# Layernorm, 32-head attention and a gated GLU on one core: Q and K projected in 120-row tiles and laid out through DRAM, and a freer choice of banks for side work

## The chip, the cores and the metric

The kernel runs on one core of one Trainium2 chip. The metric is the device time in microseconds, given as the median of three runs. Engines are named as in the profile: PE (matmuls), PEld (weight loads of PE), DVE (vector), ACT (scalar), POOL (GpSimd), SP (the engine that issues most DMAs).

## What is computed

```
xn = layernorm(x)                            # x: 2048 x 640
q, k, v = split(xn @ wqkv)                   # 32 heads of 20 columns
s = (softmax(q k^T / sqrt(20)) v) @ wo       # per head, 2048 queries by 2048 keys
g = silu((sigmoid(xn @ w_gate) * (xn @ w_up)) @ w_down)     # F = 1728
out = x + s * g
```

All inputs are bfloat16.

## The kernel before

**Blocks.** The 32 heads form 8 groups of 4, and the 2048 queries 4 chunks of 512: 32 blocks (`b`), worked through in order. In a block each of the 4 heads meets 16 key tiles of 128, so there are 64 jobs. A job is a score matmul (L559, `score_mm`; the four heads stand on four 32-row strips of PE, so up to four run beside each other), an exponential, and a value matmul (L599, into `oacc`; the heads stand on four 32-column strips).

**Two ways to the exponential.** Most jobs go to ACT (L83, `pt`), two or three score tiles at a time, from `scA0` or `scA1` (two banks each) and, for a third tile, from `bank[0]` or `bank[1]`. Some key tiles go to DVE, all four heads together: `iv` (L844, one per head, from a bank) and then four integer passes `pb` (L644), whose value matmuls use four scaled copies of V (`v`, `vs`).

**Side work on PE.** Between scores and values PE does everything else: K of the next group (`mk_k`, L354), Q of the next block (`mk_q`, L365, with the bound below, L168), V (`mk_v`, L385), the GLU (`mk_gu` L415, `mk_down` L438) and the output projection (`mk_out`, L475, only in the last blocks). Each is an `Item`: PE steps into one of the single banks, then ACT and DVE steps that read it and set the bank free. Their order is written out by a planner inside the kernel (the `while` loop in L778): it walks through an assumed time, keeps what each engine is busy with, and lets a score step, a value step or a side step be next by rules in L902 to L915. Side work takes `bank[2]`, and the two others only while it is behind a due amount (L886 to L890). `URGENT`, `ROUNDS`, `HOLD`, `SLACK`, `LEAD`, `LAG`, `D_LAST` in L29 are numbers of these rules. PE, ACT and DVE run in exactly this order; SP and POOL instructions are put in order by the framework.

**Q and K.** Four heads of 20 columns are spread to 4 x 32 columns, so that each head starts on a strip: POOL copies the weights into `wqk` (L120) with zeros in between, and a projection of a group has 128 output rows, 80 of them filled. Column 0 of each strip carries a bound: K has 1 there (`ones_r`), and Q gets minus the sum of |q| times the largest |k| of each row, by one more matmul (L168) of `aq` = |q| (ACT, L164) with `md`, which comes from the maxima of K (`k_max`, L150). DVE evacuates K into `kT` (L144) and Q into a `q` tile (L172), both in SBUF and ready for the scores.

**After a block.** DVE copies `oacc` to `on` (L612); the row sums go through DRAM (`ld`, `lt`, DVE `rt`, `rd`, `rl`, all issued by SP), POOL multiplies (`on_bf`, L629), and SP writes the heads' rows into `oU` (L637). The gate results leave DVE in two buffers `gqs` (L448) and are written to DRAM.

**End.** When all items are done, `tail_steps` projects the last 512 rows and writes them out.

Of the kernel before, what the change touches and what calls it, by code (L numbers as in the profile page):

```python
# [18 lines left out]
P = 128  # L19
# [33 lines left out]
def kernel(  # L53
# [41 lines left out]
    gq_dram = dram.tile([S, D], FP32, name="gq_dram", tag="gqd", bufs=1)  # L95

# [5 lines left out]
    wqks = [persist.tile([P, 2 * KD, GH, 32], BF16, name=f"wqk{i}") for i in range(2)]  # L102
# [5 lines left out]
    eps_t = const.tile([P, 1], FP32, name="eps_t")  # L108
    mds = [const.tile([P, P], BF16, name=f"md{i}") for i in range(2)]
# [6 lines left out]
    def load_wqk(g):  # L116
        st = wk.tile([P, KD, 2, GC], BF16, tag="wst", bufs=2, name="wst")
# [8 lines left out]
    def load_wv(pr):  # L126
        w = wk.tile([P, KD, 2 * GC], BF16, tag="wv", bufs=2, name="wv")
        nc.sync.dma_start(out=w, in_=wqkv_v[:, :, 2, pr * 2 * GC:(pr + 1) * 2 * GC])
        return w
# [32 lines left out]
    def q_abs(ps):  # L162
        aq = wk.tile([P, QC], BF16, tag="aq", bufs=1, name="aq")
        nc.scalar.activation(out=aq, in_=ps, func=ACT.Abs)  # L164
        return aq
# [4 lines left out]
    def q_evac(ps):  # L170
        q = wk.tile([P, QC], BF16, tag="q", bufs=3, name="q")
        nc.vector.tensor_scalar_mul(out=q, in0=ps, scalar1=qscale)  # L172
        return q
# [7 lines left out]
    def v_evac(ps, pr, tts):  # L181
        n = len(tts)
        src = ps[:, 0:n * 2 * GC].rearrange("p (t h e) -> p t h e", t=n, e=DH)
        nc.vector.tensor_copy(out=vts[pr % 2][:, tts[0]:tts[0] + n, :, 1:1 + DH], in_=src)
        for i, tt in enumerate(tts):
            if tt in DKT:
                vf = wk.tile([P, 2 * GC], FP32, tag="vf", bufs=2, name="vf")
# [9 lines left out]
    with tc.tile_pool(name="ln", bufs=2) as lp, \  # L197
# [17 lines left out]
        for j in range(GH):  # L215
# [6 lines left out]
                                base=31, pattern=[[32, GH], [P, 32]], channel_multiplier=-1)  # L222
        for i in range(2):
# [5 lines left out]
        aq0 = q_first = psq = None  # L229
# [36 lines left out]
        q_first = q_evac(psq)  # L266
# [47 lines left out]
    qs = {0: q_first}  # L314
# [42 lines left out]
    def mk_q(b, at):  # L357
# [13 lines left out]
        def ev():  # L371
            qs[b] = q_evac(st["ps"])
# [3 lines left out]
                     ("DVE", 0.60, ev, "free", lambda t: q_at.__setitem__(b, t))], at, pre=[("md", g)])  # L376

# [123 lines left out]
    for b in range(NBLK):  # L501
        g, c = divmod(b, NQC)
        mk = []
        if g + 1 < NG:
            mk.append(lambda at, g=g, c=c: [mk_k(g + 1, c, at)])
        if g % 2 == 1 and g + 1 < NG:
# [6 lines left out]
        if b + 1 < NBLK:  # L513
            mk.insert(min(1, len(mk)), lambda at, b=b: [mk_q(b + 1, at)])
# [43 lines left out]
    def score_mm(dst, b, kt, j):  # L558
        nc.tensor.matmul(dst, lhsT=kTs[(b // NQC) % 2][32 * j:32 * j + 32, kt * P:(kt + 1) * P],  # L559
                         rhs=qs[b][32 * j:32 * j + 32, :], start=True, stop=True, tile_position=(32 * j, 0))  # L560
# [58 lines left out]
    def norm_b(b, on, lt):  # L619
# [5 lines left out]
        rl = w2.tile([P, QC], FP32, tag="rl", bufs=2, name="rl")  # L625
# [38 lines left out]
    def tail_steps():  # L664
# [27 lines left out]
        early(mains[3], 3, slice(0, 512), False)  # L692
        tp2 = psum.tile([P, 2 * QC], BF16, name="tp2", tag="oacc")
        for i in range(4):
            nc.tensor.transpose(out=tp2[0:GC, i * P:(i + 1) * P], in_=onq[:, i, :], identity=ident)
        o7 = w2.tile([GC, QC], BF16, tag="on_bf", bufs=2, name="o7")
# [29 lines left out]
    with tc.manual_schedule(engines={ENG.PE, ENG.Activation, ENG.DVE}):  # L726
# [21 lines left out]
        active = []  # L748
        norm_pending = None
# [28 lines left out]
        while pv_block[0] < NBLK or items or glu_items or any(it.i < len(it.ops) for it in active):  # L778
# [3 lines left out]
            if bb > blk_loaded:  # L782
                blk_loaded = bb
                g, c = divmod(bb, NQC)
                if c == 0 and g + 1 < NG:
                    load_wqk(g + 1)
# [5 lines left out]
            active = [it for it in active if it.i < len(it.ops)]  # L792

# [77 lines left out]
            if free["PE"] <= now:  # L871
# [10 lines left out]
                if cur is None:  # L882
                    m_new, m_bank = None, None
# [22 lines left out]
                elif can_f and (margin < URGENT or stay is None):  # L906
# [9 lines left out]
                if nxt == "F":  # L916
# [3 lines left out]
                    d_bank = None  # L920
                    if d_can and busy <= T_F + T_MODE + PL + SLACK:
                        d_bank = next((f for f in (2, (nfill + 1) % 2, nfill % 2) if flex[f] <= now), None)
# [104 lines left out]
```

## Time and profile before

| what | value |
|---|---|
| median of three runs | 928.38 us (926.77 to 932.43) |
| the profiled execution | 926.63 us, its span 924.8 us |
| mean granted TensorE clock | 0.982 |
| PE, ACT, DVE busy | 852.2, 828.1, 751.3 us |
| POOL busy | 103.8 us |
| DMA | 54.28 MB, mean 59 GB/s |

Busy time is the time in which at least one instruction of the engine was under way. Instructions of PE and of ACT overlap, so the time of one instruction is longer than what it adds; the distance from one start to the next is what it costs in a dense stretch. In a group of instructions the row gives its line, engine, operation, output and inputs, count, busy time, mean length, then the idle time of the engine ahead of them and what ended it.

### The profile page before, as it was taken

The numbers are of one execution on the slowest core, as the hardware profiler recorded it, in microseconds if no ns is written. First come the engines' busy times: TensorE is split into PE (matmuls) and PEld (weight loads), VectorE is DVE, ScalarE is ACT, GpSimd is POOL, SyncE is SP. The second block draws the span as 40 slices with busy tenths as digits, with TensorE's granted clock in tenths as the row PEclk, the third lists the DMA queues.
The fourth block names the chain that finished last, engine by engine and source line by source line (L and its number), as shares of the span: only waits on it lengthen the run. The fifth ranks groups of instructions, "written<-read, shape, count | busy, mean of one in ns | idle before, by whom it ended". The sixth has DMA issues, their size and how long they took to land.

```text
span 924.8 us, 18739 instructions
## 1 busy us (share of the span) xinstructions
PE 852.2 (92%) x7266; PEld 294.5 (32%) x7352; DVE 751.3 (81%) x1288; ACT 828.1 (90%) x1037; POOL 103.8 (11%) x138
## 2 busy tenths in 40 slices
PE   3799999999999999999999999999999999889875
PEld 2332223343322233333222333333323333223222
DVE  8588758888778997887859888899897688998864
ACT  3799999999999999998999999999999999998760
POOL 3020100111000000111000000111000000003222
PEclk9799999999999999999999999999999999999898
DMA  8402222112121221101221211101211111213431
GB/s 224 136 11 63 63 66 62 39 32 56 43 73 35 66 62 38 32 25 29 63 73 37 74 34 36 39 13 46 62 46 38 31 39 31 93 38 112 137 96 55
DMA packets 85288, 54.28 MB, mean 59 GB/s; under 512 B 33172, under 2 KB 79060, under 8 KB 85200
## 3 DMA queue, kind: packets, MB, share of 16 engines
q1 hardware_dynamic: 83760, 51.45, 19.8%
q10 hardware_dynamic: 1440, 1.64, 0.5%
q8 instruction: 57, 0.93, 0.4%
q14 instruction: 31, 0.25, 0.1%
HBM read 42.15 MB, written 8.37 MB: 55 GB/s over the span
## 4 chain that ended last, share of the span: by engine, by line
PE 49%; ACT 23%; DVE 18%; issue 6%; DMA 2%; SPq 1%; POOL 0%; DVEq 0%; ACTq 0%; POOLq 0%
PE oacc L599 13%; PE scA_431 L559 7%; PE scA_430 L559 6%; DVE pb L644 6%; DVE iv L844 6%; PE bk_434 L415 4%; PE bk_432 L415 3%; PE bk_433 L415 3%; PE bk_433 L438 2%; PE bk_432 L438 1%; PE bk_434 L475 1%; PE bk_434 L438 1%; PE bk_432 L365 1%; PE bk_434 L354 1%; DVE stats L236 1%
## 5 line engine op out<-in xcount | busy, mean ns | idle before, releaser
L644 DVE TENSOR_SCALAR pb<-iv 128x2048 int16<-128x2048 int16 x440 | 304.1, 715 | 2.8
L844 DVE TENSOR_SCALAR iv<-bk_434 128x512 int16<-128x512 f32 x182 | 124.5, 684 | 39.8 <-PE bk_434 L559 39.4
L844 DVE TENSOR_SCALAR iv<-bk_433 128x512 int16<-128x512 f32 x131 | 89.4, 683 | 29.6 <-PE bk_433 L559 29.3
L844 DVE TENSOR_SCALAR iv<-bk_432 128x512 int16<-128x512 f32 x127 | 86.6, 682 | 23.1 <-PE bk_432 L559 22.8
L629 POOL TENSOR_TENSOR on_bf<-on,rl 128x512 bf16<-128x512 f32 x31 | 42.7, 1378 | 537.0 <-DMA rl<-rd 365.4
L599 PE MATMUL oacc<-pb,vs_74 128*21 128x512 bf16 x684 | 86.8, 392 | 2.8 <-DVE pb L644 2.6
L559 PEld LDWEIGHTS <-kT_69 32*128 32x128 bf16 x1024 | 38.4, 91 | 130.0 <-issue 125.3
L559 PEld LDWEIGHTS <-kT_70 32*128 32x128 bf16 x1024 | 40.1, 91 | 124.0 <-issue 117.5
L559 PE MATMUL scA_430<-q,kT_69 32*128 32x512 bf16 x367 | 73.3, 386 | 2.9 <-DVE q L172 0.8
L559 PE MATMUL scA_431<-q,kT_70 32*128 32x512 bf16 x362 | 71.1, 385 | 4.0 <-ACT pt_10982 L83 0.7
L559 PE MATMUL scA_430<-q,kT_70 32*128 32x512 bf16 x357 | 71.0, 386 | 3.2 <-ACT pt_10810 L83 0.5
L559 PE MATMUL scA_431<-q,kT_69 32*128 32x512 bf16 x359 | 71.1, 385 | 1.8 <-ACT pt_1526 L83 0.3
L599 PE MATMUL oacc<-pb,vs_73 128*21 128x512 bf16 x636 | 70.4, 381 | 0.5 <-issue 0.3
L415 PE MATMUL bk_434<-xnT,wgu 128*128 128x512 bf16 (+1 forms) x224 | 68.4, 383 | 1.2 <-issue 0.8
L415 PEld LDWEIGHTS <-wgu 128*128 128x128 bf16 (+1 forms) x560 | 43.3, 98 | 75.8 <-issue 54.0
L438 PEld LDWEIGHTS <-hT 128*128 128x128 bf16 x448 | 35.9, 97 | 46.8 <-issue 38.1
L415 PE MATMUL bk_432<-xnT,wgu 128*128 128x512 bf16 (+1 forms) x155 | 47.6, 383 | 2.0 <-DVE iv L844 1.0
L599 PEld LDWEIGHTS <-v_72 128*21 128x21 bf16 x1024 | 31.4, 91 | 47.5 <-issue 36.8
L559 PE MATMUL bk_433<-q,kT_70 32*128 32x512 bf16 x114 | 44.4, 389 | 0.1
L415 PE MATMUL bk_433<-xnT,wgu 128*128 128x512 bf16 (+1 forms) x142 | 42.8, 383 | 1.9 <-issue 0.8
L559 PE MATMUL bk_433<-q,kT_69 32*128 32x512 bf16 x108 | 41.6, 385 | 0.0
L559 PE MATMUL bk_432<-q,kT_69 32*128 32x512 bf16 x103 | 39.9, 388 | 0.0
(1780 smaller groups left out, 2150.4 us busy)
## 6 DMA issues: line engine op xcount, KB each, us to landing
rl<-rd SPq DMA_DIRECT2D x124, 64.0 KB
wgu<-in_B_w_gate_dram SPq DMA_DIRECT2D x24, 320.0 KB
wgu<-in_B_w_up_dram SPq DMA_DIRECT2D x24, 320.0 KB
gq_dram<-gqs SPq DMA_DIRECT2D x32, 160.0 KB
ob<-gq_dram SPq DMA_DIRECT2D x12, 320.0 KB
oU<-on_bf SPq DMA_DIRECT2D x108, 20.0 KB
wd<-in_B_w_down_dram SPq DMA_DIRECT2D x1, 2080.0 KB
ob<-in_A_x_dram SPq DMA_DIRECT2D x12, 160.0 KB
```

Source lines behind the costliest of these rows:

```text
L236: nc.vector.bn_stats(out=stats[:, h, :], in_=xt[:, i, h * HD:(h + 1) * HD])
L354: nc.tensor.matmul(ps, lhsT=wslice(g, 1, kd), rhs=xnT[:, kd, c * 512:(c + 1) * 512], start=(kd == 0), stop=(kd == KD - 1))
L365: nc.tensor.matmul(st["ps"], lhsT=wslice(g, 0, kd), rhs=xnT[:, kd, c * QC:(c + 1) * QC], start=(kd == 0), stop=(kd == KD - 1))
L415: nc.tensor.matmul(st[key][0:fs, :], lhsT=w[:, i, kd, ko * P:ko * P + fs], rhs=xnT[:, kd, c * QC:(c + 1) * QC], start=(kd == 0), stop=(kd ...
L438: nc.tensor.matmul(st["ps"][:, 0:HD], lhsT=hT[0:fsz[kf], kf, t4 * P:(t4 + 1) * P], rhs=wd[0:fsz[kf], kf, h * HD:(h + 1) * HD], start=(kf = ...
L475: nc.tensor.matmul(st["ps"][:, 0:HD], lhsT=oU[:, kd, tt * P:(tt + 1) * P], rhs=wo[:, kd, h * HD:(h + 1) * HD], start=(kd == 0), stop=(kd = ...
L559: nc.tensor.matmul(dst, lhsT=kTs[(b // NQC) % 2][32 * j:32 * j + 32, kt * P:(kt + 1) * P], rhs=qs[b][32 * j:32 * j + 32, :], start=True, s ...
L599: nc.tensor.matmul(oacc[32 * j:32 * j + DH + 1, :], lhsT=lhsT, rhs=u["src"], start=first, stop=last, tile_position=(0, 32 * j), skip_group ...
L629: nc.gpsimd.tensor_tensor(out=on_bf, in0=on, in1=rl, op=ALU.mult)
L644: nc.vector.tensor_scalar(out=pb[:, k, :, :].bitcast(I16), in0=iv, scalar1=0.25, scalar2=cst, op0=ALU.mult, op1=ALU.add)
L844: nc.vector.tensor_scalar(out=d["iv"][:, j, :], in0=bank[bk], scalar1=I_OFF, scalar2=I_LOW, op0=ALU.add, op1=ALU.max)
```

## The change

Groups 0 and 1 (heads 0 to 7) keep the old way. Heads 8 to 31 form four units `u` of six heads, 120 columns. The weights of a unit are loaded as they are (`load_wu`, no copy on POOL). K of a chunk (`mk_ku`) and Q of a chunk (`mk_qu`) are projected into 120 rows, evacuated by DVE into a small tile (`ku`, `qu`, one ring of two buffers) and written to DRAM (`kD`, `qD`). The bounds of a unit, for all four chunks, come from four matmuls into four 32-column strips of one bank (`mk_bu`), and go to DRAM too (`bD`). `load_kT` and `load_q` then read each head's 20 rows to their strip in `kT` and in one of three fixed `q` tiles. The numbers of the planner change, side work may take any bank once all scores are claimed or when neither a value nor a score step is possible (`FALL`), and in `tail_steps` a transpose moves ahead of five matmuls and four additions move back. Some buffers shrink from two to one (`wst`, `wv`, `vf`, `rl`).

```diff
-URGENT, ROUNDS, HOLD, SLACK, LEAD, LAG, D_LAST, D_LAST_END = 0.15, 3, 0.15, 0.8, 40.0, 8.0, 16, 0
+PG = 2
+UH = 6
+UC = UH * DH
+
+URGENT, ROUNDS, HOLD, SLACK, LEAD, LAG, D_LAST, D_LAST_END = 0.15, 4, 0.0, 0.1, 20.0, -5.0, 20, 0
+D_ORD, M_ORD, WAIT3, FALL = 0, 1, 0.0, 1
...
+    qts = [persist.tile([P, QC], BF16, name=f"q{i}") for i in range(3)]
...
-        aq = wk.tile([P, QC], BF16, tag="aq", bufs=1, name="aq")
+        aq = wk.tile([P, QC], BF16, tag="aq", bufs=4, name="aq")
...
+    def load_wu(u):
+        w = wk.tile([P, 2 * KD, GH, 32], BF16, tag="wp", bufs=2, name="wu")
...
+        for i in range(2):
+            nc.sync.dma_start(out=w[:, :, i, :], in_=wqkv_v[:, :, i, f0:f0 + UC])
...
+    def mk_ku(u, c, at):
...
+        def ev():
+            st["k"] = wk.tile([P, QC], BF16, tag="ku", bufs=2, name="ku")[0:UC, :]
+            nc.vector.tensor_copy(out=st["k"], in_=st["ps"][0:UC, :])
+            nc.sync.dma_start(out=kD[u][:, c * QC:(c + 1) * QC], in_=st["k"])
...
+        return Item([("PE", alloc, [(T_MM, lambda kd=kd: u_mm(st, u, 1, c, kd)) for kd in range(KD)]),
+                     ("DVE", 0.60, ev, "free", mark("kD", u, c)), ("DVE", 0.60, mx, "", end)], at,
+                    pre=[("wu", u)])
...
+    def mk_qu(u, c, at):
...
+            q = wk.tile([P, QC], BF16, tag="ku", bufs=2, name="qu")[0:UC, :]
+            nc.vector.tensor_scalar_mul(out=q, in0=st["ps"][0:UC, :], scalar1=qscale)
+            nc.sync.dma_start(out=qD[u][:, c * QC:(c + 1) * QC], in_=q)
...
+    def mk_bu(u, at):
...
+            for c in range(NQC):
+                nc.tensor.matmul(st["ps"][32 * c:32 * c + UH, :], lhsT=mku[u][2], rhs=aqs[(u, c)][0:UC, :],
+                                 start=True, stop=True, tile_position=(0, 32 * c), skip_group_check=True)
...
+            bt = wk.tile([P, QC], BF16, tag="ku", bufs=2, name="bt")
...
+    def load_kT(g):
+        for u, o, j, n in spans(g):
+            for i in range(n):
+                r = 32 * (j + i) + 1
+                nc.sync.dma_start(out=kTs[g % 2][r:r + DH, :], in_=kD[u][(o + i) * DH:(o + i + 1) * DH, :])
...
+    def load_q(b):
...
+                nc.sync.dma_start(out=qts[b % 3][r:r + DH, :], in_=qD[u][(o + i) * DH:(o + i + 1) * DH, cs])
+            nc.sync.dma_start(out=heads(qts[b % 3])[j:j + n, 0, :], in_=bD[u][o:o + n, cs])
...
+        for u in range(NU):
+            first = (PG + u * UH // GH - 1) * NQC
+            if first <= b < first + 3:
+                if b == first:
+                    mk.append(lambda at, u=u: [mk_ku(u, i, at) for i in range(NQC)])
+                if b == first + 1:
+                    mk.append(lambda at, u=u: [mk_qu(u, i, at) for i in range(NQC)] + [mk_bu(u, at)])
...
-        early(mains[3], 3, slice(0, 512), False)
         tp2 = psum.tile([P, 2 * QC], BF16, name="tp2", tag="oacc")
         for i in range(4):
             nc.tensor.transpose(out=tp2[0:GC, i * P:(i + 1) * P], in_=onq[:, i, :], identity=ident)
+        early(mains[3], 3, slice(0, 512), False)
...
+            if k_next < NG and base() >= (k_next - 1) * NQC and all(
+                    ev_at.get(("kD", u, c), 1e9) <= now for u, _, _, _ in spans(k_next) for c in range(NQC)):
+                load_kT(k_next)
+                k_at[k_next] = now + 5.5
...
+            if q_next < NBLK and base() >= q_next - 2:
...
+                    load_q(q_next)
+                    q_at[q_next] = max(now + 5.0, k_at[q_next // NQC])
...
-                        for f in ((2, (nfill + 1) % 2, nfill % 2) if behind else (2,)):
+                        for f in ((2,) if not behind and claimed[0] < NJOB * NBLK and not (FALL and not pv_ok and not can_f) else [(2, 1 - own, own), (2, own, 1 - own)][M_ORD]):
```

In the changed file the score matmul is L689, the value matmul L729, the unit's projection L402, its bounds L462, the evacuations of K, Q and bounds L413, L448 and L467, the writes L414, L449 and L469, the reads of K L490 and of Q L498 and L499, and the output projection L598.

On PE, early in the program, before: a projection of K for group 1 (`wqk`, 128 output rows) between value weights and values. Each matmul has its weight load in the row above it.

```order
L385 LDWEIGHTS xnT
L385 MATMUL bk_433<-wv,xnT 128x160
L354 LDWEIGHTS wqk_76
L354 MATMUL bk_434<-xnT,wqk_76 128x512
L354 LDWEIGHTS wqk_76
L354 MATMUL bk_434<-xnT,wqk_76 128x512
```

And now, in block 4, the first projection of unit 0 (`wu`, 120 output rows), with a score step in its midst:

```order
L402 LDWEIGHTS wu
L402 MATMUL bk_451<-xnT,wu 120x512
L402 LDWEIGHTS wu
L402 MATMUL bk_451<-xnT,wu 120x512
L689 LDWEIGHTS kT_82
L689 MATMUL scA_449<-q_95,kT_82 128x512
L689 LDWEIGHTS kT_82
L689 MATMUL scA_449<-q_95,kT_82 128x512
L689 LDWEIGHTS kT_82
L689 MATMUL bk_450<-q_95,kT_82 128x512
L402 LDWEIGHTS wu
L402 MATMUL bk_451<-xnT,wu 120x512
```

The step itself is the same; there are fewer of them, and K of six heads goes into a bank that then leaves for DRAM instead of `kT`.

On SP, where block 3 has ended and `ld`, `lt`, `rd`, `rl` and `oU` carry its row sums, with the writes of K of unit 0 now among them and the reads into `kT` behind them:

```order
L744 DMA ld<-on 4x512
L746 DMA lt<-ld 128x16
L414 DMA kD_67<-ku 120x512 x2
L754 DMA rd<-rt 128x16
L414 DMA kD_67<-ku 120x512
L757 DMA rl<-rd 32x512 x4
L414 DMA kD_67<-ku 120x512
L767 DMA oU<-on_bf 20x512 x4
L490 DMA kT_81<-kD_67 20x2048 x4
```

Before, a block's queue held these rows (here from block 4's `rl` to block 5's `lt`) with at most writes of `gqs` and loads of weights among them:

```order
L627 DMA rl<-rd 32x512 x4
L450 DMA gq_dram<-gqs 128x320
L637 DMA oU<-on_bf 20x512 x2
L637 DMA oU<-on_bf 8x512
L637 DMA oU<-on_bf 12x512
L637 DMA oU<-on_bf 20x512
L450 DMA gq_dram<-gqs 128x320
L614 DMA ld<-on 4x512
L450 DMA gq_dram<-gqs 128x320
L616 DMA lt<-ld 128x16
```

The writes of K stand in the same queue as the row sums, and each is released by DVE's evacuation.

On PE, at the end of the last block, before: the last value matmuls (`pt`, ACT's exponentials) and behind them output projections, all into `bk_434` (32 of them in this way).

```order
L599 LDWEIGHTS v_72
L599 MATMUL oacc<-pt_11783,v_72 21x512
L475 LDWEIGHTS oU
L475 MATMUL bk_434<-wo,oU 128x320
L475 LDWEIGHTS oU
L475 MATMUL bk_434<-wo,oU 128x320
```

And now, with the last DVE tile's values (`pb`) and 13 output projections behind them, in banks `bk_452`, `bk_451` and `bk_450`:

```order
L729 LDWEIGHTS vs_86
L729 MATMUL oacc<-pb,vs_86 21x512
L598 LDWEIGHTS oU
L598 MATMUL bk_452<-wo,oU 128x320
L598 LDWEIGHTS oU
L598 MATMUL bk_452<-wo,oU 128x320
L598 LDWEIGHTS oU
L598 MATMUL bk_452<-wo,oU 128x320
L598 LDWEIGHTS oU
L598 MATMUL bk_451<-wo,oU 128x320
```

More of the output projections have moved ahead of the last values, and the rest no longer share one bank.

More of the change, by code (lines that the diff above doesn't have):

```diff
@@ new lines, with alloc, ab, ev @@
+    aqs = {}
+    def mk_qu(u, c, at):
+        st = {}
+        def alloc():
+            st["ps"] = misc_ps()
+        def ab():
+            aqs[(u, c)] = q_abs(st["ps"])
+        def ev():
+            q = wk.tile([P, QC], BF16, tag="ku", bufs=2, name="qu")[0:UC, :]
+            nc.vector.tensor_scalar_mul(out=q, in0=st["ps"][0:UC, :], scalar1=qscale)
+            nc.sync.dma_start(out=qD[u][:, c * QC:(c + 1) * QC], in_=q)
+        return Item([("PE", alloc, [(T_MM, lambda kd=kd: u_mm(st, u, 0, c, kd)) for kd in range(KD)]),
+                     ("ACT", 0.48, ab, "", mark("aq", u, c)),
+                     ("DVE", 0.60, ev, "free", mark("qD", u, c))], at, pre=[("bD", u - 1)] if u else [])
@@ L695, in tail_steps @@
             nc.tensor.transpose(out=tp2[0:GC, i * P:(i + 1) * P], in_=onq[:, i, :], identity=ident)
+        early(mains[3], 3, slice(0, 512), False)
+        o7 = w2.tile([GC, QC], BF16, tag="on_bf", bufs=2, name="o7")
+        nc.vector.tensor_copy(out=o7, in_=tp2[0:GC, 0:QC])
+        for t4 in range(4):
+            late_mm(mains[t4], t4, slice(0, 512))
+        rest = bank[2]
+        for t4 in range(4):
+            dst = rest[:, t4 * EX:(t4 + 1) * EX]
+            early(dst, t4, slice(512, D), False)
+            late_mm(dst, t4, slice(512, D))
@@ L905 @@
                     nxt = "PV"
-                elif can_f and (margin < URGENT or stay is None):
+                elif can_f and (margin < URGENT or (stay is None and not (flex[nfill % 2] <= now + WAIT3 and flex[nfill % 2] > now and margin > WAIT3))):
                     nxt = "F"
```

162 lines of the change are left out of this document (143 added, 19 removed).

## The prediction, made before the changed kernel ran

> **What bounds the kernel now.** I read the busy shares first, then the slices, then busy time by stage, then single rows for what one step costs.
>
> ```profile
> PE 852.2 (92%) x7266; PEld 294.5 (32%) x7352; DVE 751.3 (81%) x1288; ACT 828.1 (90%) x1037; POOL 103.8 (11%) x138
> ...
> PE   3799999999999999999999999999999999889875
> ...
> ACT  3799999999999999998999999999999999998760
> PEclk9799999999999999999999999999999999999898
> ```
>
> No engine stands out. PE is at 90% or more in slices 3 to 34, ACT in slices 3 to 36 but one, and both fall off after that. By stage (columns: window, its length, then busy us of PE, PEld, DVE, ACT, POOL, granted clock, DMA share, GB/s):
>
> ```profile
> 500.00:600.00 100.00, 97.41 (x875) 34.09 (x881) 85.68 (x146) 97.33 (x124) 7.10 (x8) 1.00 0.14 42
> 100.00:766.00 666.00, 645.44 (x5558) 220.80 (x5628) 550.62 (x919) 637.52 (x797) 58.20 (x67) 1.00 0.17 47
> 766.00:794.00 28.00, 25.46 (x223) 7.85 (x222) 23.95 (x43) 25.13 (x32) 1.26 (x1) 0.94 0.28 90
> 794.00:816.00 22.00, 18.89 (x179) 5.63 (x179) 21.21 (x36) 21.84 (x29) 1.64 (x1) 1.00 0.11 29
> 816.00:890.00 74.00, 63.59 (x575) 20.70 (x574) 64.54 (x107) 64.89 (x77) 17.73 (x19) 0.93 0.32 98
> ```
>
> From 100 to 766 PE is 96.9% busy and ACT 95.7%. From 794 to 816 PE has almost no side work left: PE falls to 86% and ACT rises to 99.3%. So ACT can run nearly without gaps when PE has time to spare; where PE is full, ACT's gaps are scores that come late. From 100 to 890 ACT is busy 637.52 + 25.13 + 21.84 + 64.89 = 749.4 of 790 us: 40.6 us of gaps is what a lighter PE could win back.
>
> A matmul's busy time overstates PE, so I take its cost from the distance between starts (start, length, instruction):
>
> ```profile
> 299.58 1.04 PE L415 MATMUL bk_434<-xnT,wgu 128*128 128x512 bf16 x4
> 300.55 0.39 PE L559 MATMUL scA_431<-q,kT_69 32*128 32x512 bf16 x2
> ...
> 301.78 0.59 PE L599 MATMUL oacc<-pt_3858,v_72 128*21 128x512 bf16 x3
> 302.00 0.38 PE L599 MATMUL oacc<-pt_3868,v_72 128*21 128x512 bf16 x2
> 302.21 0.38 PE L599 MATMUL oacc<-pt_3895,v_72 128*21 128x512 bf16 x2
> ...
> 302.53 0.39 PE L559 MATMUL scA_431<-q,kT_69 32*128 32x512 bf16 x2
> ...
> 302.85 0.39 PE L599 MATMUL oacc<-pb,v_72 128*21 128x512 bf16 x2
> ```
>
> Four projections take 1.04 us, the last of them about 0.38: (1.04 - 0.38)/3 = 0.22 us a step. Value steps (up to four beside each other) start at 301.78, 302.00 and 302.21: 0.22 again. From scores to values, 302.53 to 302.85, it is 0.32: a change of kind costs 0.10 more.
>
> ACT in the same way:
>
> ```profile
> 299.87 0.62 ACT L164 ACTIVATE aq<-bk_433 128x512 bf16<-128x512 f32 x1
> 300.34 1.05 ACT L83 ACTIVATE pt_3895<-scA_430 128x1024 bf16<-128x1024 f32 x1
> 301.25 1.07 ACT L83 ACTIVATE pt_3906<-scA_431 128x1024 bf16<-128x1024 f32 x1
> 302.15 1.08 ACT L83 ACTIVATE pt_3920<-scA_430 128x1024 bf16<-128x1024 f32 x1
> 303.06 0.67 ACT L83 ACTIVATE pt_3936<-bk_433 128x512 bf16<-128x512 f32 x1
> 303.55 1.09 ACT L83 ACTIVATE pt_3936<-scA_431 128x1024 bf16<-128x1024 f32 x1
> ```
>
> A pair of score tiles costs 0.905 us (300.34 to 302.15 is two), a single one or an absolute value 0.48 (0.47 and 0.49).
>
> **The change, part by part.** *Projections.* Before, groups 2 to 7 need 6 x 4 chunks x (5 K + 5 Q + 1 bound) = 264 PE steps. After, four units need 4 x 4 x 10 = 160, and each unit's four bound matmuls stand in four column strips beside each other, as the value steps do: 4 more. 100 steps go, 22.0 us at 0.22. The group row gives an upper end.
>
> ```profile
> L365 PE MATMUL bk_432<-xnT,wqk_75 128*128 128x512 bf16 x25 | 7.4, 382 | 0.6 <-issue 0.6
> L415 PE MATMUL bk_434<-xnT,wgu x224: 376/379/403, 73.3 to 720.1; 128*128 128x512 bf16 x106, 128*64 128x512 bf16 x6
> ```
>
> 7.4/25 = 0.30 us each, with the ends of runs in it, would make it 30 us; I take 22.0, since PE is paced by starts. The second row holds matmuls with 128 and with 64 weight columns, and all last 376 to 403 ns: a 120-column one costs what a 128-column one costs, and only the number of them counts. The Trainium skill ("Trainium Kernel Development and Optimization", Best Practices) says always to tile to 128 partitions, which speaks against 120 rows: by it 160 steps would be 6% short of full, an estimate of 2 us lost; the row shows that what was paid before was whole steps with 80 useful rows of 128.
>
> *What the new order does to the rest.* Counted in the two orders: exponentials of two tiles go from 722 to 702, of one tile from 164 to 216; value matmuls from 3368 to 3332; DVE tiles from 110 to 107; changes of kind on PE from 1495 to 1505. On PE that is 20 x 0.22 = 4.4 us of score steps and 36/4 x 0.22 = 2.0 us of value steps less, 1.0 us of changes more. **PE: -22.0 - 4.4 - 2.0 + 1.0 = -27.4 us.** **ACT:** -20 x 0.905 + 52 x 0.48 - 8 x 0.48 (absolute values, 32 to 24) = **+3.0 us**.
>
> *DVE* loses 12 `iv` and 12 `pb`, 8 K evacuations, 8 maxima, and 4 on the Q side net: 44 x about 0.7 = 31 us.
>
> ```profile
> L644 DVE TENSOR_SCALAR pb<-iv 128x2048 int16<-128x2048 int16 x440 | 304.1, 715 | 2.8
> L844 DVE TENSOR_SCALAR iv<-bk_434 128x512 int16<-128x512 f32 x182 | 124.5, 684 | 39.8 <-PE bk_434 L559 39.4
> ```
>
> DVE's idle time is scores that are not there yet, so I count this at nothing: DVE was 660.3 of 790 us busy between 100 and 890, and PE and ACT cover it. The six POOL copies of weights go, and nobody waited for them.
>
> *The way through DRAM.* SP issues 717 rows for 522, and four cost 1.72 us (below): 195 x 0.43 = 84 us more on SP, 2.6 us a block. Q is loaded two blocks before it is read and K a group before; a block takes nearly 29 us at most (924.8/32), against a landing time of about 2 us:
>
> ```profile
> SPq L616 <- DMA ld<-on: 28.7, 26, 1.9
> ...
> 71.39 0.33 SPq L624 DMA_DIRECT2D rd<-rt  x1
> 72.81 1.72 SPq L627 DMA_DIRECT2D rl<-rd  x4
> ...
> 77.72 3.08 SPq L637 DMA_DIRECT2D oU<-on_bf  x4
> ```
>
> (`lt` waited for `ld` to land 1.9 us at the longest.) So the reads are hidden: 0. If that cover went, 24 blocks would pay 2 us each, 48 us. The writes are another matter. `ku`, `qu` and `bt` share two buffers, so a third evacuation on DVE waits until the first has been written out, and behind it stand `iv` and `pb`, and PE behind those. The gate output is written the same way today, from two buffers:
>
> ```profile
> DVE gqs L448 <- ACT td L83: 4.0, 6, 1.2
> ```
>
> That is the only wait those 32 instructions show, and it is for ACT, not for a write. In the new order at least three DVE instructions (2.1 us) stand between an evacuation and the second one after it. I take 0, and keep as upper end a stall at each of the 8 runs of four writes.
>
> *End.* The chain of waits ends so:
>
> ```profile
> 897.66 0.39 PE bk_434 L475 x2
> ...
> 898.15 0.50 DVE ob L482
> ...
> 898.69 0.85 PE bk_434 L475 x5
> ...
> 899.63 0.50 DVE ob L482
> ...
> 900.17 0.85 PE bk_434 L475 x5
> ...
> 906.10 0.84 PE bk_434 L475 x5
> ```
>
> After the last value step one bank serves all output projections: PE, then DVE, then PE, 1.48 us a round (898.69 to 900.17), until 906.94. The new order lets them take any bank once all scores are claimed: 13 of these matmuls are left behind the last value step, where 32 were (two, then six rounds of five), and they alternate banks, so PE runs on: 13 x 0.17 = 2.2 us for the 9.3 from 897.66. **-7 us.** From 0 (the values of the last DVE tile, now interleaved, come no earlier) to -9.
>
> **How much of PE's 27.4 us becomes time.** If ACT kept its gaps: nothing. If ACT ran at 99.3%: 790 - 752.4/0.993 = 32. PE's own saving is 27.4, so all of it fits in ACT only without gaps. I take the best long window of before, 500 to 600, where ACT ran at 97.3%: (749.4 + 3.0)/0.973 = 773, **-17 us**. The sum against the profiled execution: 926.63 - 17 - 7 = 902.6. The median of the runs lies 1.75 us above that execution: **904**.
>
> **Rivals.**
> 1. *PE is the bound and everything follows it*: 926.6 - 27.4 - 7 + 1.75 = 894. For it: ACT's 99.3% with a light PE. Against: ACT would need 98.6% over 763 us.
> 2. *ACT is the bound already*: then PE's steps are idle time and ACT's +3 is paid: 926.6 + 3 - 7 + 1.75 = 924. For it: 95.7% busy at 0.905 us back to back. Against: the 99.3% stage. The Trainium skill ("Perfetto Trace Analysis", Identifying the Most-Contended Engine) holds matmul busy time to be no measure of PE's headroom and weight-load busy time to be one; PEld's 32% would make PE far from full and ACT, at 90%, the engine to relieve, which is this rival. Its half about matmul busy time the trace bears out (382 ns a row, 220 ns a step); its other half counts no change of kind, and some 1500 of these at 0.10 are 150 us of PE.
> 3. *Slower: DVE stalls behind SP.* Place: the writes of `kD` and `qD` stand in SP's queue between `rd` and `oU`, a run that lasted from 71.39 to 80.80, 9.4 us. If a K or Q write falls behind it, the next but one evacuation holds DVE. Eight runs of four writes, up to 9.4 us each: 75 us, 904 + 75 = 979 at worst; at 5 us each 944. It decides from 24/8 = 3 us each. For it: order rows with `kD` in the midst of that run. Against: `gqs`.
> 4. *The change doesn't do what it says*: side work stays in bank 2. The order shows 759 of 1722 side matmuls on bank 2 where it was 709 of 1810, so more of them stay there; but the end does alternate. It would take the 7 us away: 911.
>
> **How the numbers follow.** Forecast with rival 4 beside it: 0.54, its own range 897 to 913. Rival 1: 0.15 (889 to 897). Rival 2: 0.20 (914 to 930). Rival 3: 0.11 (925 to 979). 1% of 928.4 is 9.3, and a difference within that can't be told from none; the border is 919.1. Faster: 0.54 + 0.15 + 0.06 of rival 2 = 0.75; same: 0.14 of rival 2 and 0.03 of rival 3 = 0.17; slower: 0.08. The range from 889 to 928 leaves out the dear half of rival 3 and little else; its low end is ACT at 99.3% throughout and the shorter end (926.6 - 32 - 7 + 1.75), its high end the time of before, where neither PE's saving nor the end brings anything.
>
> **What would show it.** PE's busy time falls by 27 us or more; ACT's stays within 5 us of 828, and its share from 100 to the end of the scores rises from 95% to 97%. The new `ku`, `qu`, `bt` on DVE show under 5 us of waits for DMA in all, and the scores of blocks 8 to 31 none for `q` and `kT`. At the end the output projections change banks, and the stretch in which ACT has nothing left is shorter by some 7 us. I am wrong if ACT's share stays at 95% (rival 2), or if DVE shows long waits ahead of L413, L448 or L467, or PE ahead of L689 for DMA (rival 3).

## The result, and the profile after

The changed kernel takes **890.0 us** (median of four runs, 888.51 to 892.73) against 927.6 us for the kernel before on the same chip: a ratio of 0.9589, 95% interval [0.9546, 0.9633]. The forecast was 904 with a range of 889 to 928. The direction and the range held, at the range's low end; the gain is 38 us where 24 were forecast.

The busy shares and the slices of the changed kernel:

```profile
PE 830.5 (93%) x7173; PEld 291.9 (33%) x7228; DVE 720.6 (81%) x1240; ACT 822.6 (93%) x1061; POOL 91.5 (10%) x135
...
PE   3699999999999999999999999999999999978886
...
ACT  4699999999999999999999999999999999999870
```

PE shows 21.7 us less busy time, DVE 30.7, ACT 5.5. PE's figures are somewhat low: every matmul has its weight load, and the pages list 7352 weight loads before and 7228 after, but 7266 and 7173 matmuls, so 86 and 55 matmul records are missing. The shares hardly show a change, since the span shrank with the work. One long window tells more (window, its length, then busy us of PE, PEld, DVE, ACT, POOL, granted clock, DMA share, GB/s). Before:

```profile
100.00:800.00 700.00, 676.63 (x5839) 230.38 (x5913) 580.29 (x970) 668.65 (x835) 59.47 (x68) 1.00 0.17 48
```

and after:

```profile
100.00:800.00 700.00, 681.00 (x5968) 234.12 (x6012) 581.93 (x974) 688.20 (x883) 50.42 (x63) 1.00 0.23 64
```

ACT's share rises from 95.5% to 98.3%. It is the number to follow through the experiments.

The second view is a ruler laid along the work: the windows are cut where a quarter of the 2048 score matmuls has started (the counts scatter by a few, since a cut can fall a score step early), so each row is about the same amount of scores. Of the score matmuls alone, before:

```profile
0.00:256.20 256.20, 71.22 (x512) 18.65 (x512) 0.98 0.27 72
256.20:471.60 215.40, 71.24 (x512) 18.86 (x514) 1.00 0.17 47
471.60:680.80 209.20, 70.34 (x512) 19.77 (x512) 1.00 0.16 46
680.80:891.10 210.30, 69.59 (x515) 18.70 (x515) 0.97 0.22 65
```

and after:

```profile
0.00:240.60 240.60, 71.01 (x510) 19.24 (x511) 0.99 0.28 75
240.60:450.70 210.10, 71.38 (x520) 19.36 (x515) 1.00 0.23 62
450.70:658.00 207.30, 69.89 (x512) 17.86 (x512) 1.00 0.23 62
658.00:864.00 206.00, 69.31 (x513) 18.29 (x513) 0.97 0.28 81
```

The quarters are shorter by 15.6, 5.3, 1.9 and 4.3 us, 27.1 in all (14.5, 7.9, 1.6 and 3.0 when cut at the exact start of the 513th, 1025th and 1537th score matmul and the end of the last). More than half of it lies in the first quarter. That quarter varies by itself: the run "The end by itself" below has the order of the kernel before in it and took 264.3 us for it where the kernel before took 257.4, at a lower clock (0.955 against 0.980). A run below shows that the planner's new numbers and choice of banks shorten that quarter by 10.3 us without any unit.

The end, in the chain of waits (start, length, instruction):

```profile
869.84 0.33 PE oacc L729 x4
870.16 0.51 PE bk_452 L598 x3
870.68 0.68 PE bk_451 L598 x5
871.36 0.68 PE bk_450 L598 x5
872.04 0.05 issue
872.09 2.42 PE scA_449 L868 x9
```

The 13 output projections (L598) that are left alternate over three banks and take 1.88 us. The last value step ends at 870.16, where it ended at 897.66, and from there to the span's end it is 19.0 us (889.12 - 870.16) where it was 27.1 (924.79 - 897.66).

### The profile page after: what moved, and what is told of

It reads as the page before. It is cut to its first block, busy times and chain, and to the rows that moved or that the text cites. A ratio compares the mean times of both kernels' runs of the same rounds, so it can differ in the third digit from the quotient of the medians.

```text
span 889.1 us, 18834 instructions
## 1 busy us (share of the span) xinstructions
PE 830.5 (93%) x7173; PEld 291.9 (33%) x7228; DVE 720.6 (81%) x1240; ACT 822.6 (93%) x1061; POOL 91.5 (10%) x135
## 4 chain that ended last, share of the span: by engine, by line
PE 43%; ACT 35%; DVE 11%; issue 5%; DMA 3%; SPq 1%; POOL 0%; ACTq 0%; DVEq 0%; POOLq 0%
PE oacc L729 12%; PE scA_449 L689 6%; PE scA_448 L689 6%; PE bk_452 L538 4%; DVE pb L774 4%; DVE iv L1060 3%; PE bk_451 L561 2%; PE bk_450 L538 2%; PE bk_452 L402 2%; ACT tnh L87 2%; PE bk_451 L402 1%; DVE stats L249 1%; PE bk_452 L561 1%; PE bk_450 L561 1%; PE bk_451 L538 1%
## 5 line engine op out<-in xcount | busy, mean ns | idle before, releaser
L774 DVE TENSOR_SCALAR pb<-iv 128x2048 int16<-128x2048 int16 x428 | 297.0, 714 | 2.5
L1060 DVE TENSOR_SCALAR iv<-bk_452 128x512 int16<-128x512 f32 x167 | 113.9, 682 | 35.1 <-PE bk_452 L689 34.6
L1060 DVE TENSOR_SCALAR iv<-bk_450 128x512 int16<-128x512 f32 x137 | 93.3, 681 | 29.3 <-PE bk_450 L689 29.1
L1060 DVE TENSOR_SCALAR iv<-bk_451 128x512 int16<-128x512 f32 x124 | 84.4, 681 | 23.6 <-PE bk_451 L689 23.4
L729 PE MATMUL oacc<-pb,vs_86 128*21 128x512 bf16 x660 | 83.4, 387 | 2.4 <-DVE pb L774 2.0
L538 PE MATMUL bk_452<-xnT,wgu 128*128 128x512 bf16 (+1 forms) x274 | 80.7, 383 | 1.7 <-issue 1.0
L689 PEld LDWEIGHTS <-kT_81 32*128 32x128 bf16 x1024 | 38.2, 91 | 131.1 <-issue 127.8
L689 PEld LDWEIGHTS <-kT_82 32*128 32x128 bf16 x1024 | 39.1, 91 | 116.7 <-issue 108.6
L729 PE MATMUL oacc<-pb,vs_85 128*21 128x512 bf16 x624 | 70.6, 381 | 0.5 <-DVE pb L774 0.3
L729 PEld LDWEIGHTS <-v_84 128*21 128x21 bf16 x1024 | 30.5, 91 | 45.5 <-issue 36.4
L729 PEld LDWEIGHTS <-v_83 128*21 128x21 bf16 x1024 | 29.0, 90 | 43.5 <-issue 33.5
L538 PE MATMUL bk_450<-xnT,wgu 128*128 128x512 bf16 x140 | 40.5, 382 | 0.8 <-issue 0.6
L729 PE MATMUL oacc<-pb,v_84 128*21 128x512 bf16 x220 | 34.7, 382 | 2.2 <-DVE pb L774 1.7
L561 PE MATMUL bk_451<-wd,hT 128*128 128x320 bf16 (+1 forms) x168 | 33.4, 303 | 0.0
L729 PEld LDWEIGHTS <-vs_86 128*21 128x21 bf16 x660 | 22.3, 91 | 25.1 <-issue 17.6
L538 PE MATMUL bk_451<-xnT,wgu 128*128 128x512 bf16 (+1 forms) x99 | 29.2, 383 | 1.1 <-issue 0.6
L729 PE MATMUL oacc<-pb,v_83 128*21 128x512 bf16 x208 | 30.2, 383 | 0.0
L689 PE MATMUL scA_448<-q_94,kT_81 32*128 32x512 bf16 x134 | 27.4, 387 | 1.4 <-DVE q_94 L181 0.8
L689 PE MATMUL scA_448<-q_95,kT_82 32*128 32x512 bf16 x130 | 26.2, 387 | 2.0 <-ACT pt_11716 L87 1.0
```

Of the source, the lines that this page charges most:

```text
L538: nc.tensor.matmul(st[key][0:fs, :], lhsT=w[:, i, kd, ko * P:ko * P + fs], rhs=xnT[:, kd, c * QC:(c + 1) * QC], start=(kd == 0), stop=(kd ...
L561: nc.tensor.matmul(st["ps"][:, 0:HD], lhsT=hT[0:fsz[kf], kf, t4 * P:(t4 + 1) * P], rhs=wd[0:fsz[kf], kf, h * HD:(h + 1) * HD], start=(kf = ...
L729: nc.tensor.matmul(oacc[32 * j:32 * j + DH + 1, :], lhsT=lhsT, rhs=u["src"], start=first, stop=last, tile_position=(0, 32 * j), skip_group ...
L774: nc.vector.tensor_scalar(out=pb[:, k, :, :].bitcast(I16), in0=iv, scalar1=0.25, scalar2=cst, op0=ALU.mult, op1=ALU.add)
L1060: nc.vector.tensor_scalar(out=d["iv"][:, j, :], in0=bank[bk], scalar1=I_OFF, scalar2=I_LOW, op0=ALU.add, op1=ALU.max)
```

## The experiments

The forecast charged the units' PE work and treated the planner's new numbers only through the order that came out. The first four runs ask whether that is how the gain arises. P stands for "PE is the bound and its steps are paid", A for "ACT is the bound", R for "the rules decide".

### The units with the old numbers and the old choice of banks

```diff
-URGENT, ROUNDS, HOLD, SLACK, LEAD, LAG, D_LAST, ... = 0.15, 4, 0.0, 0.1, 20.0, -5.0, 20, 0
+URGENT, ROUNDS, HOLD, SLACK, LEAD, LAG, D_LAST, ... = 0.15, 3, 0.15, 0.8, 40.0, 8.0, 16, 0
-for f in ((2,) if not behind and claimed[0] < NJOB * NBLK and not (FALL and ...) else [...]):
+for f in ((2, (nfill + 1) % 2, nfill % 2) if behind else (2,)):
```

> The units and their way through DRAM as in the changed kernel, with the planner's numbers and its bank rule as before. Theory P (PE's steps set the pace, each step saved is time saved): PE's steps counted in this order come to 24.6 us less than before, the end keeps its one bank, so about 903. Rival R (the new numbers and bank rule made room, the units alone win half of their steps): 913 to 918. Rival N (the units win nothing without the rules): 925 or more.

Measured: 922.56 us against 929.56, ratio 0.9912 [0.9878, 0.9946]: 8 us by the ratio, a fifth of the gain. None of the three theories named it; it lies between R and N. The same window:

```profile
100.00:800.00 700.00, 671.81 (x5873) 229.72 (x5921) 590.83 (x981) 666.30 (x826) 49.18 (x62) 1.00 0.23 63
```

ACT stays at 95.2%, so most of what PE saved did not reach ACT. (PE's 671.8 us against 676.6 before say little: by the weight loads, 48 and 74 matmul records are missing in the two windows.)

### The new numbers and choice of banks, without the units

The same two edits the other way round, on the kernel before.

> The kernel before with the new numbers and the new bank rule, and no units. Theory P: PE's steps come to 4 us less in this order and the end is about 7 us shorter, so 915 to 917. Rival R: 905 or less, since the rules alone close ACT's gaps. Rival A (ACT is the bound in either kernel): ACT's starts come to 12 us more here, so 930 or more.

Measured: 925.31 us, ratio 0.9950 [0.9928, 0.9972]. The rules alone gain 5 us; this too lies outside all three theories. The ruler shows why so little:

```profile
0.00:245.90 245.90, 71.53 (x514) 19.73 (x514) 0.97 0.26 70
245.90:460.50 214.60, 69.87 (x512) 18.61 (x512) 1.00 0.17 46
460.50:677.10 216.60, 72.25 (x516) 19.65 (x516) 1.00 0.19 51
677.10:895.60 218.50, 68.76 (x512) 18.74 (x512) 0.95 0.23 66
```

The first quarter is 10.3 us shorter than before, the third and fourth 7.4 and 8.2 us longer (the fourth in part by the granted clock, 0.95 against 0.97). Side work that the first quarter no longer does comes later and is paid there. Units alone 8 us, rules alone 5, both 38: some 25 us exist only together.

### 96 PE steps less, under the old rules

The kernel before, in which Q of groups 2 to 7 is summed over one of its five slices: 24 x 4 = 96 projection steps fewer, and nothing else of the change. The planner writes its order anew for it, as in every run here but the one with one buffer.

```diff
+nk = KD if g < 2 else 1
-for kd in range(KD)
+for kd in range(nk)
```

> The kernel before, with Q of heads 8 to 31 taken from one of its five weight slices (96 PE steps left out, so its output is not the reference's); nothing else of the change. Theory P: PE's steps come to 23 us less, so about 905. Rival A: ACT has as much to do as before or some 5 us more, so 925 to 932. Rival R: half, about 915.

Measured: 931.38 us, ratio 1.0012 [0.9984, 1.0039]. No gain; the time is the one that theory A named. The same window:

```profile
100.00:800.00 700.00, 669.51 (x5748) 225.21 (x5814) 574.63 (x956) 674.81 (x843) 59.08 (x68) 0.99 0.19 51
```

PE has 99 weight loads fewer in it than before (5814 against 5913), and ACT's share is 96.4%. Two things stand beside the missing gain. The granted clock was lower: 0.965 in the mean of the ten runs against 0.979 for the kernel before, which is worth some 7 us of the 23 (an estimate, worked out in the last section). And the planner gave DVE 107 key tiles instead of 110 and ACT their 12 jobs: ACT is 832.7 us busy, 828.1 before. So the run shows that the time did not fall, not that the 96 steps were worth nothing.

### 96 PE steps more, under the new rules

The changed kernel with three more matmuls in each of the 32 unit projections (the first slice is written three times over before the sum begins).

```diff
-for kd in range(KD)
+for kd in range(-3, KD)      # below 0: slice 0 with start=True
```

> The changed kernel with three more matmuls ahead of each of the 32 unit projections (96 PE steps whose sums are overwritten). Theory P: PE's steps come to 24 us more than in the changed kernel, so about 914. Rival A: ACT's starts are 4 us less, so 886 to 892. Rival R: the rules hide half, about 902.

Measured: 916.7 us, ratio 0.9856 [0.981, 0.9902]. By the ratios (0.9856/0.9589) that is 2.8% or 25 us over the changed kernel, 0.26 us for each step added, where theory P named 24.

```profile
100.00:800.00 700.00, 685.56 (x5963) 237.33 (x6009) 580.24 (x968) 668.58 (x839) 49.79 (x62) 1.00 0.22 61
```

PE is full (97.9%) and ACT is back at 95.5%, where it was before the change. PE's weight loads fill 34% of this window. The Trainium skill ("Perfetto Trace Analysis", Identifying the Most-Contended Engine) tells the reader to judge TensorE's headroom by weight-load busy time, beside the share of the peak matmul rate. As a sign of headroom the measurement goes against it here: at that 34% a PE step more costs its full time.

### 96 PE steps less, under the new rules

The two edits before last together: the rules-only kernel with one slice for Q of groups 2 to 7. No units, so DVE keeps its work and Q and K stay in SBUF.

> The kernel before with the new numbers and the new bank rule, and 96 projection steps left out: Q of groups 2 to 7 is summed over one of five slices (so those Q values differ). No units, so DVE keeps its work. The rules alone gave 925.3 us and the 96 steps alone 931.4 against 929.6, which is nothing. Theory C (the old rules kept PE's saving from ACT; with the new rules each step left out counts): 925.3 less 96 x 0.22 to 0.28 = 898 to 904 us. Theory U (what counts is the units' own placement and DVE's 44 instructions fewer): 920 to 926 us.

Measured: 905.88 us, ratio 0.9743 [0.9689, 0.9796]. Against the rules alone (0.9743/0.9950) that is 2.1% or 19 us, 0.20 us a step, where the same edit under the old rules brought no gain.

```profile
100.00:800.00 700.00, 687.71 (x5965) 228.66 (x5967) 593.48 (x989) 687.07 (x878) 57.00 (x69) 0.99 0.19 51
```

ACT reaches 98.2% without a unit in the kernel. So fewer PE steps under the new rules win 19 of the 33 us that the units win under them (0.9950 to 0.9589), without the way through DRAM and with DVE 733.7 us busy (751.3 before, 720.6 in the changed kernel). The other 14 us are not explained by the number of steps, which is nearly the same; some 4 of them go with the clock (0.975 in the mean of the runs here, 0.983 in the changed kernel), and the rest is open. That 906 lies a little above the forecast 898 to 904 is within what its interval allows.

Where the 96 steps come off tells much of the difference between the two orders. The table counts the side steps on PE (neither score nor value) in each quarter of the scores, by their weight loads, of which the traces miss none:

| kernel | quarter 1 | 2 | 3 | 4 |
|---|---|---|---|---|
| before | 543 | 447 | 434 | 310 |
| the same, 96 steps less | 515 | 433 | 439 | 256 |
| rules only | 475 | 465 | 473 | 326 |
| the same, 96 steps less | 457 | 439 | 441 | 306 |
| changed kernel | 432 | 470 | 437 | 321 |

Under the old rules 54 of the 96 come off the last quarter and 37 off the first three; under the new ones it is 20 and 76. Late in the span PE has time to spare; the first of the two runs with 96 steps less shows PE 82% busy here and ACT 97%:

```profile
750.00:800.00 50.00, 40.87 (x356) 12.03 (x355) 34.16 (x56) 48.71 (x66) 2.57 (x2) 0.92 0.27 85
```

At 0.22 us a step, 37 steps are 8 us and 76 are 17, as an estimate; measured were 0 (with some 7 us lost to the clock) and 19.

### Which half of the rules

Three runs put old values back into the changed kernel: all numbers (with the new choice of banks), only `LEAD` and `LAG`, only `HOLD` and `SLACK`.

```diff
-URGENT, ROUNDS, HOLD, SLACK, LEAD, LAG, D_LAST, ... = 0.15, 4, 0.0, 0.1, 20.0, -5.0, 20, 0
+URGENT, ROUNDS, HOLD, SLACK, LEAD, LAG, D_LAST, ... = 0.15, 3, 0.15, 0.8, 40.0, 8.0, 16, 0   # all
+URGENT, ROUNDS, HOLD, SLACK, LEAD, LAG, D_LAST, ... = 0.15, 4, 0.0, 0.1, 40.0, 8.0, 20, 0    # lead, lag
+URGENT, ROUNDS, HOLD, SLACK, LEAD, LAG, D_LAST, ... = 0.15, 4, 0.15, 0.8, 20.0, -5.0, 20, 0  # hold, slack
```

> The changed kernel with its bank rule but the old numbers (rounds 3, hold 0.15, slack 0.8, lead 40, lag 8, last DVE tile at 16). Both halves of the old rules with the units gave 922.6, the changed kernel 890. If the bank rule makes the gain: 890 to 897 us. If the numbers make it: 914 to 922 us. If each gives a part: between, near 905.

> The changed kernel with two of its numbers as before: lead 40 and lag 8, which pace the side work against the scores. All numbers of before together cost 22 us (912.2 against 890). If the pacing is what kept side work from PE's idle time: 905 to 912 us. If it is hold, slack and rounds: 889 to 895 us.

> The changed kernel with hold 0.15 and slack 0.8 as before (how long PE stays idle for a slot that is about to come free, and how long DVE prefers another step to a conversion). If these hold PE back: 905 to 912 us. If the pacing does: 889 to 895 us.

Measured: 912.19 (0.9825 [0.9763, 0.9887]), 912.15 (0.9813 [0.9784, 0.9843]) and 903.7 us (0.9735 [0.971, 0.9759]). By the ratios, against the changed kernel: +22, +21 and +14 us. The numbers are the larger half (22 of the 30 us between the units with all old rules and the changed kernel), the choice of banks the smaller (8), taken in this order; the new numbers with the old choice of banks were not run. Of the numbers both pairs matter, and they don't add up. The last run, at 903.7, lies between its two cases. The pair `LEAD` and `LAG`:

```profile
0.00:256.40 256.40, 73.43 (x514) 19.37 (x514) 0.97 0.27 74
256.40:466.80 210.40, 70.75 (x514) 19.65 (x514) 1.00 0.24 65
466.80:673.80 207.00, 70.13 (x512) 18.94 (x512) 1.00 0.23 62
673.80:888.20 214.40, 69.74 (x513) 18.24 (x513) 0.91 0.24 70
```

The first quarter is as long as before the change (256.4), the second and third as short as after it. The last is 8.4 us longer, for which its lower granted clock is enough (0.91 against 0.97 over 214 us is 13 us), so the loss that the trace ties to the two numbers is the first quarter's 15.8, of which the lower clock there (0.97 against 0.99) may be 3 to 5 us. Side work stands further ahead of the scores in this order: 530 side steps in the first quarter where the changed kernel has 432. The two numbers don't do that by themselves, though: with all numbers old and the new choice of banks, `LEAD` and `LAG` included, it is 464. Over all runs the first quarter goes with this count: in the kernel before, the units under the old rules, the 96 steps less under the old rules, the end by itself and the old `LEAD` and `LAG` it holds 515 to 543 side steps and ends at 256 to 264 us; in all others it holds 428 to 475 and ends at 240 to 251. It is a relation over the runs, not a test by itself. The run with all old numbers belongs to the second group and is as slow as that with the old `LEAD` and `LAG` (912.2), so the first quarter is not the only way to lose the time.

### More work for ACT

The changed kernel, |Q| taken three times in each unit chunk instead of once. The planner is told of it (1.44 us for the step instead of 0.48).

```diff
 aqs[(u, c)] = q_abs(st["ps"])
+nc.scalar.activation(out=aqs[(u, c)], in_=st["ps"], func=ACT.Abs)
+nc.scalar.activation(out=aqs[(u, c)], in_=st["ps"], func=ACT.Abs)
```

> The changed kernel, the absolute value of Q taken twice more on ScalarE in each of the 16 unit chunks: 32 ACT instructions more of 0.71 us each (678 to 742 ns in the groups of the changed kernel), 23 us. Theory B2 (after the change both engines are full: 98.3% of ACT's time from 100 to 800 us is work, so ACT's time is paid too): 908 to 914 us. Theory P (PE alone sets the pace now, ACT fits in beside it): 890 to 898 us.

Measured: 902.38 us, ratio 0.9716 [0.9671, 0.9761]: +12 us by the ratios, between the two theories. ACT's instructions overlap, so the 32 added 16.5 us of busy time and not 23; against that, 12 is about three quarters:

```profile
PE 842.8 (94%) x7240; PEld 295.8 (33%) x7240; DVE 729.8 (81%) x1248; ACT 839.1 (93%) x1096; POOL 95.9 (11%) x135
```

The window of 100 to 800 us:

```profile
100.00:800.00 700.00, 683.06 (x5959) 235.83 (x5958) 581.09 (x969) 693.51 (x902) 52.74 (x63) 1.00 0.23 62
```

ACT's share goes to 99.1%. After the change both engines are close to full, and work added to either is paid: in these two runs wholly on PE and to about three quarters on ACT.

### One buffer for the way to DRAM

The changed kernel with one buffer for `ku`, `qu` and `bt`. The instructions and their order on PE, ACT and DVE are those of the changed kernel, so only waits can differ.

```diff
-wk.tile([P, QC], BF16, tag="ku", bufs=2, ...)
+wk.tile([P, QC], BF16, tag="ku", bufs=1, ...)
```

> The changed kernel with one buffer in place of two for ku, qu and bt, so that each evacuation waits until the one before has been written to DRAM. If the write's landing is covered by the distance between evacuations (as with two): 888 to 895 us. If the ring is close to stalling DVE (the forecast's third rival): 900 us and more, with DMA waits ahead of L413, L448 and L467.

Measured: 910.2 us, ratio 0.9798 [0.9751, 0.9845], +19 us by the ratios. DVE's waits (total us, times, longest):

```profile
DVE qu L448 <- DMA qD<-qu: 13.2, 6, 4.1
...
DVE bt L467 <- DMA qD<-qu: 4.0, 2, 2.8
...
DVE ku L413 <- DMA kD<-ku: 2.6, 5, 0.9
```

This is the second of the two cases expected. 13.2 + 4.0 + 2.6 = 19.8 us of waiting for DMA, and 19 us of time, although DVE is 79% busy. In the changed kernel the waits of the three are for ACT; this is the main one:

```profile
DVE qu L448 <- ACT aq L174: 8.9, 7, 1.9
```

That 19.8 and 19 agree does not mean that each microsecond is paid once. PE stands behind these evacuations for 11.1 us in all, most of it here, where it was 0.9 in the changed kernel:

```profile
PE bk L689 <- DVE qu L448: 7.3, 3, 4.1
```

And the granted clock falls around three of PE's gaps, of 1.9, 1.3 and 4.1 us, to half for 6.8, 3.4 and 6.8 us. Two of the three, with the first gap ending at 195.0 and the last lasting from 611.3 to 615.4:

```profile
190.00:204.00 14.00, 11.63 (x85) 4.44 (x78) 8.66 (x16) 10.06 (x12) 1.98 (x6) 0.76 0.24 54
608.00:622.00 14.00, 9.71 (x87) 3.74 (x84) 7.47 (x13) 8.14 (x10) 2.25 (x4) 0.76 0.14 36
```

Between 60 and 780 us these are the only stretches below 1.00, and the changed kernel has none there. They take 8.5 us of granted clock. A gap of 2.1 us at 502.8 was followed by no such stretch.

### The end by itself

The kernel before, side work free to take any bank once all scores are claimed.

```diff
-for f in ((2, (nfill + 1) % 2, nfill % 2) if behind else (2,)):
+for f in ((2, (nfill + 1) % 2, nfill % 2) if behind or claimed[0] >= NJOB * NBLK else (2,)):
```

> The kernel before, in which side work may take any bank once all scores are claimed, and nothing else: the end of the forecast by itself. By the forecast: 7 us less, 921 us against 928, with the time from the last value step to the span's end at 20 us where it was 27.1. If the order of the end matters no more than the banks do: 926 to 929 us.

Measured: 923.27 us, ratio 0.9934 [0.9911, 0.9957], 6.1 us of the 7 forecast. The last value steps and what follows them:

```profile
903.50 1.99 PE oacc L599 x19
905.49 4.18 PE bk L475 x30
909.67 2.47 PE scA L671 x10
```

The thirty output projections that remain take 4.18 us on alternating banks, 0.14 us each, and the stretch from the last value step to the span's end is 22.0 us (927.50 - 905.49) instead of 27.1. This profiled execution was the longest of the six runs, so its length is not the 923; the end's length can be read from it.

### Less work for ACT

A version meant to beat both kernels: |Q| of the units from DVE's SBUF copy.

```diff
-aqs[(u, c)] = q_abs(st["ps"])                       # ACT, from PSUM
+nc.vector.tensor_scalar(out=aqs[(u, c)][0:UC, :].bitcast(I16), in0=st["q"].bitcast(I16),
+                        scalar1=0x7FFF, scalar2=None, op0=ALU.bitwise_and)
-nc.vector.tensor_scalar_mul(out=bt, in0=st["ps"], scalar1=qscale)
+nc.vector.tensor_copy(out=bt, in_=st["ps"])
```

> The changed kernel, with the absolute value of Q in the 16 unit chunks taken by DVE from the evacuated SBUF copy (a bit mask on 120x512 int16) in place of ACT from PSUM: ACT loses 16 instructions of 0.71 us, 11.4 us; DVE gains 16 that I estimate at 0.25 us from its 128x2048 int16 pass of 0.715 us, 4 us. Theory B2 (both engines are full; 23 us more on ACT cost 12.4): half of 11.4, so 883 to 886 us, faster than both kernels. Theory P (PE alone is the pace, and ACT's 23 us only disturbed the order): 889 to 892 us.

Measured: 896.39 us, ratio 0.9649 [0.9624, 0.9674]: some 6 us slower than the changed kernel, against both expectations.

```profile
PE 836.9 (94%) x7192; PEld 292.1 (33%) x7192; DVE 713.4 (80%) x1232; ACT 821.5 (92%) x1050; POOL 93.5 (11%) x135
```

ACT lost 16 instructions and is as busy as before (821.5 against 822.6): in the order that the planner wrote for it, DVE has 104 key tiles where it had 107, and ACT took their 12 jobs. The relief was given back inside the plan. Why the result is slower and not equal is not settled. PE is not busier: its 836.9 us are of a trace without a missing matmul, and the complete trace of the changed order ("One buffer for the way to DRAM") has 843.2.

## Why the prediction was right, and which term was mis-sized

| term | forecast | measured |
|---|---|---|
| PE | -27.4 | -21.7 busy, with records missing; -25.2 between the complete traces of "The end by itself" (868.4) and "One buffer" (843.2) |
| ACT | +3.0, by starts | -5.5 busy |
| DVE (no price) | -31 | -30.7 |
| way through DRAM | 0 | no DMA wait ahead of L413, L448, L467 |
| up to the last value step | -17 | -27.5 (897.66 to 870.16) |
| end | -7 | -8.2 in the changed kernel, -6.1 by itself |
| profiled execution | -24 | -35.8 (926.63 to 890.88) |

**The mis-sized term is "how much of PE's 27.4 us becomes time".** The working took ACT's best long window of before, 97.3%, as its ceiling; ACT ran at 98.3%, and up to the last value step 27.5 us were won where 17 were forecast. ACT's +3.0 is not refuted by its busy time: ACT has 24 instructions more, as counted (1061 against 1037), but a pair that lasts 1.05 us or more costs 0.905 from start to start, so busy time falls when instructions close up and overlap. Rival 1, to which the forecast gave 0.15, named 894 and is nearest in number: the 27.5 us before the end are PE's 27.4. That is an agreement of numbers; its mechanism, PE as the one bound, is not what the runs show, since ACT's added work was paid to three quarters.

But the reason behind that term was incomplete in a way its size doesn't show. The forecast took it that a lighter PE fills ACT's gaps. Under the old rules it hardly does: 96 steps less brought no gain, some 7 us of clock aside, and the units alone 8 us, where the same way of adding up had given 24.6. Under the new rules the steps are worth 0.20 (taken out) to 0.26 us (put in), around the forecast's 0.22. The planner's numbers, which the forecast priced only through counts of instructions, make the difference together with the choice of banks, and they move side work out of the first quarter. That the forecast's range held with this condition unnamed is luck in part: the change happened to bring the rules along. A count of instructions cannot show that; the order, read by how many side steps stand ahead of each quarter of the scores, could have.

**Rival 2** (ACT is the bound already) falls for the change as a whole, since ACT's share did not stay at 95%. **Rival 3** (DVE behind SP's writes) did not come about; its mechanism is real, and the second buffer is what keeps it away: with one, 19 us. Its price of one microsecond per microsecond of waiting came out in the sum, but by PE's standing and a lower clock together. **Rival 4** falls: the projections at the end alternate banks, and the choice of banks is worth 6 us at the end by itself, and 8 in all with the units and the old numbers.

Of the signs named ahead: ACT's share rose further than the 97% named, its busy time left the 5 us band by a little (5.5), PE's fell by less than 27, DVE's waits for DMA at the three lines are none, no score matmul (L689) waits for a DMA, and the end is shorter by 8.

What stays open: which of the planner's numbers does it, since `HOLD` with `SLACK` and `LEAD` with `LAG` each cost most of what all numbers cost together, and single numbers weren't tried; the 14 us by which the changed kernel is ahead of the rules with 96 steps less; and how much of each difference is the granted clock.

## What to carry to other kernels

Before pricing a saving on one engine, test on the chip whether the present order can use it: leave out a hundred steps, look at the time, and count in which stretch of the new order they are missing. Where a written-out order couples two engines, a leaner stage and a retuned order can each be worth a per cent and be worth four together, so judge them together. A ruler of equal work (quarters of the scores) finds where time went, when busy shares of 92% to 94% look alike.

## What the runs showed of the hardware

The granted clock dipped at different depths late in the span: between 750 and 850 us it was 0.97 in the profiled executions of the kernel before and the changed one, and 0.86 with the old `LEAD` and `LAG`, which is 14 us of granted time lost in that stretch against 3. What sets the depth was not tried.

Runs of one and the same kernel differ with the mean granted clock: the kernel before took 924.29 us at 0.984 and 935.75 at 0.967, and a line fitted to all 118 runs of the record, each kernel on each chip about its own mean, gives 4.9 us for each 0.01. By this estimate the lower mean clock of a run, against the kernel that it is compared with, is worth some 7 us in the runs with 96 steps less under the old rules and with one buffer, 6 with the old `LEAD` and `LAG`, 4 with the units under the old rules and with all old numbers, and 3 with 96 steps more, with the old `HOLD` and `SLACK` and with |Q| on DVE. Whether the clock fell because of the edit was not tested; with one buffer the dips stand at PE's gaps.

The integer mask on DVE took 0.352 us for 120x512, where I had estimated 0.25 from the 128x2048 pass of 0.715:

```profile
L451 DVE TENSOR_SCALAR aq<-qu 120x512 int16<-120x512 int16 x16 | 5.6, 352 | 0.1
```
